# Window attention with a 3x3 depthwise position term: value-first slot order, earlier projection, and 30 channels convolved two blocks ahead

## The chip, the cores and the metric

The kernel runs on one core of a Trainium2 chip. The metric is the device time of one execution in microseconds (us). The core has five engines with queues of their own that work in order: TensorE (PE in the profile, with weight loads shown as PEld), VectorE (DVE), ScalarE (ACT), GpSimd (POOL) and SyncE (SP). Here SP only issues DMA transfers. Engines wait for one another through semaphores.

## The reference, cut to what matters

The input is an image of 511 x 511 positions with 192 channels in bfloat16. It is cut into 73 x 73 windows of 7 x 7 = 49 positions, and attention with 4 heads of 48 channels runs inside each window.

```python
pe = jnp.zeros_like(x)
for i in range(kk):                  # kk = 3, zero padding of 1
    for j in range(kk):
        pe = pe + xp[:, i:i + H, j:j + W, :] * dw_pe[i, j][None, None, None, :]
x0 = x + pe
h = _layernorm(x0, axis=-1)
...                                  # 73 x 73 windows of 49 positions
qkv = (hw @ w_qkv).reshape(-1, ws * ws, 3, nh, dh)
attn = jnp.einsum('wnhd,wmhd->whnm', q, k) * scale
attn = _softmax(attn, axis=-1)
out = jnp.einsum('whnm,wmhd->wnhd', attn, v)
out = out.reshape(-1, ws * ws, C) @ w_o
...
return x0 + out
```

## The kernel before

**Blocks.** Windows lie on partitions: up to 128 of them make a block. `_blocks` lists "halves" of 64 windows, two to a block. The first 73 halves are rows of windows (columns 0 to 63). The next 9 are columns of windows (columns 64 to 72, window rows 0 to 63). The 9 x 9 windows of the remaining corner make a last, smaller block. That gives 42 blocks: 0 to 35 of row halves, 36 with one of each, 37 to 40 of column halves, and 41 the corner with 81 windows.

**Tiles of a block.** `XP` (one buffer) holds the padded 9 x 9 patch of every window, 81 partitions x 128 windows x 192 channels. `X` (three buffers, block b in `X[b % 3]`) holds the 49 positions of every window; the convolution is added to it in place, later the attention's result, and it is stored from there. `HO` (two buffers) holds the normalized input with channels on partitions, and later, in the same place, the attention's output. `h` (two buffers) is the normalized input of seven positions before its transpose.

**Work for block b+1, done while block b is in attention.** Convolution: one matmul for each channel, `XP` against a table `T` (81 x 49) of that channel's weights, into `psc` (L314); after ten channels DVE adds the result to `X` (L320). Normalization, in seven rows of seven positions: statistics on DVE (L325), then on POOL a scale (L334), a power of -0.5 (L335) and the product (L337), which gives `h`. Then 14 transposes on TensorE into two `psc` buffers (L347), copied to `HO` by DVE and ACT (L357).

**Attention, in slots.** A slot handles one group of eight windows; a full block has 16 slots, the corner block 11. The letters are those of the code:

- A (`stage_A`, twice): q, then k, matmuls L369 into `ps`, each copied by ACT (L377), which is where most convolution matmuls are mixed in, by `fill`
- E (`stage_E`): transposes the result of two slots ago (L452), copied to `HO` by DVE (L453)
- `proj`: output projection of the block before, four positions at a time, 13 for a block (L464). ACT copies it to `pO` (L475, L477) and POOL adds it to `X` (L479)
- the transposes L347 of the next block, if one is due
- D (`stage_D`): the attention weights of the slot before times v (L428); DVE takes the reciprocal of the sums and scales (L437, L438)
- B (`stage_B`): scores (L407), whose exponential ACT writes to `pt` (L415)
- V (`stage_V`): v for this slot (L385), copied by ACT (L393)

The order of this list is the order of the slot, and all engines' queues are filled in that order (the schedule is written out by hand). `ps` has three buffers and `psc` two, each taken in rotation.

**Due times.** In the main loop, f is the share of the block's slots that is done at the end of a slot, and `part(lo, hi, total)` says how much of a list of `total` pieces is due when f goes from `lo` to `hi`. Convolution, projection, statistics, transposes, `XP` loads and `X` loads of block b+2 each have such a pair. `hook(share)`, called at five places in a slot, issues what is due of the statistics, stores and loads. Stores of a block's rows follow its projections. All loads and stores are issued on SP's queue: `XP` at L236 (nine patch columns for each half, more where a half touches the image's edge and is cut), clears of padding at L198, `X` at L250, stores at L299. `XP` loads for block b+2 start only when the convolution of block b+1 is done.

**Start.** `XP` is set to zero, weights are folded and a check of the logits' size is computed, the first loads are placed, and a branch picks `fast` (the path that runs) or `slow`. `fast` then convolves and normalizes block 0 before the first slot.

Of the kernel before, what the change touches and what calls it, by code (L numbers as in the profile page):

```python
# [41 lines left out]
def _blocks(nwr, nwc):  # L42

    full, tall = min(_HALF, nwc), min(_HALF, nwr)
    halves = [(a, 0, 0, 1, full) for a in range(nwr)]
    halves += [(0, b, 1, 0, tall) for b in range(full, nwc)]
    blocks = [[h + (64 * i,) for i, h in enumerate(halves[k : k + 2])] for k in range(0, len(halves), 2)]
    if nwc > full:
        cur, p = (blocks.pop(), 64) if len(halves) % 2 else ([], 0)
        for a in range(tall, nwr):  # L50
            n = nwc - full
            if p + n > BLK:
                blocks.append(cur)
                cur, p = [], 0
            cur.append((a, full, 0, 1, n, p))
            p += n
        if cur:
            blocks.append(cur)
    return blocks


class _Kernel:
    def __init__(self, ctx, tc, x, dw_pe, w_qkv, w_o, out, eps, logit_lim):
# [12 lines left out]
        nc.vector.memset(self.XP[:, 0:88, :], 0.0)  # L76
        nc.gpsimd.memset(self.XP[:, 88:BLK, :], 0.0)
        self.ident = consts.tile([128, 128], BF, name="ident")
        self.zero = consts.tile([16, C], BF, name="zero")
        nc.vector.memset(self.zero[:], 0.0)  # L80
        self.T = big.tile([128, C, S], BF, name="T")
        self.X = [big.tile([128, S, C], BF, name=f"X{i}") for i in range(3)]
# [3 lines left out]
        gi = consts.tile([1, 1], I32, name="gi")  # L86

# [89 lines left out]
        counts = [max(ln[4] + ln[5] for ln in blk) for blk in _blocks(self.NWR, self.NWC)]  # L177
        for i, t in enumerate(self.X):
            if len(counts) <= i or counts[i] < BLK:
                nc.gpsimd.memset(t[:], 0.0)  # L180
        for t in list(self.load_xp(0)) + list(self.load_x(0)):
            t()
# [19 lines left out]
    def load_xp(self, b):  # L202

        nc, x, XP, XPr, W, NWR, NWC = self.nc, self.x, self.XP, self.XPr, self.W, self.NWR, self.NWC
        blocks, clear, dram = _blocks(NWR, NWC), self.clear, self.dram
        for a0, b0, da, db, n, p0 in blocks[b]:
            left = [0] if b0 == 0 else []
            right = [] if b0 + (n - 1) * db < NWC - 1 else list(range(n)) if da else [n - 1]
            if left and any(ln[1] for bb in blocks[:b] for ln in bb):
                yield clear(XPr[0], p0, n if da else 1)  # L210
            if right and b:
                yield clear(XPr[8], p0 + right[0], len(right))
            last = a0 + (n - 1) * da
            cuts = [0] + ([1] if da and a0 == 0 else []) + ([n - 1] if da and last == NWR - 1 else []) + [n]
            for i, j in zip(cuts, cuts[1:]):
                if j <= i:
                    continue
                top, bot = a0 + i * da == 0, a0 + (j - 1) * da == NWR - 1
                if top and b:
                    yield clear(XP[0:9], p0 + i, j - i)  # L220
                if bot and b:
                    yield clear(XP[KP - 9 : KP], p0 + i, j - i)
                pr0, pr1 = (1 if top else 0), (8 if bot else 9)
                for pc in range(9):
                    q, sh = (WS - 1, -1) if pc == 0 else (0, 1) if pc == 8 else (pc - 1, 0)
                    n0, n1 = i, j
                    if pc == 0 and left:
                        n0 = j if da else i + 1
                    if pc == 8 and right:
                        n1 = i if da else j - 1  # L230
                    if n1 <= n0:
                        continue
                    dims = [[W * C, pr1 - pr0], [WS * C * (W * da + db), n1 - n0], [1, C]]
                    dst = XPr[pc, pr0:pr1, p0 + n0 : p0 + n1, :]
                    src = dram(x, WS * (a0 + n0 * da) - 1 + pr0, WS * (b0 + n0 * db + sh) + q, dims)
                    yield lambda dst=dst, src=src: nc.sync.dma_start(out=dst, in_=src)  # L236
# [7 lines left out]
    def load_x(self, b):  # L244

        nc = self.nc
        for r0, r1 in ((0, 4), (4, WS)):
            for p, at in self.strips(b, r0, r1):
                dst = self.X[b % 3][p, r0 * WS : r1 * WS, :].rearrange("p (r q) c -> p r (q c)", q=WS)
                yield lambda dst=dst, src=self.dram(self.x, *at): nc.sync.dma_start(out=dst, in_=src)  # L250


    def fast(self, ctx):
# [7 lines left out]
        tmp1 = pool.tile([128, S], F32, name="tmp1")  # L261
        expo = pool.tile([128, S], F32, name="expo")
# [3 lines left out]
        v_ = pool.tile([128, 4, NH, S], BF, name="v")  # L266
# [7 lines left out]
        for t in (pt, v_):  # L274
            nc.vector.memset(t[:], 1.0)
# [54 lines left out]
        def ln_norm(b, r, eng):  # L330

            t = slice(r * WS, (r + 1) * WS)
            e = nc.gpsimd
            e.tensor_scalar(out=tmp1[:, t], in0=bnst[:, t, 2], scalar1=1.0 / C, scalar2=self.eps, op0=ALU.mult, op1=ALU.add)  # L334
            e.tensor_tensor(out=rstd[:, t], in0=tmp1[:, t], in1=expo[:, t], op=ALU.pow)  # L335
            h = hr.next()
            eng.tensor_tensor(  # L337
                out=h[:], in0=self.X[b % 3][:, t, :], in1=rstd[:, t].unsqueeze(2).to_broadcast([128, WS, C]), op=ALU.mult
            )
            return h  # L340
# [38 lines left out]
        def stage_V(b, ck, fill, eng):  # L379
# [39 lines left out]
        def stage_D():  # L419
# [68 lines left out]
        class Next:  # L488
# [16 lines left out]
            def stats(n_, goal):  # L505
                while n_.si < goal and len(n_.ready) - n_.tr < 2:
                    n_.items[n_.si]()
                    n_.si += 1
# [19 lines left out]
        sq = []  # L528

        for g in range(NG + LE + 1):  # L530
# [6 lines left out]
            if ck == 0:  # L537
                n = Next(b + 1) if b + 1 < NB else None
# [8 lines left out]
            if 1 <= b and ck >= LE:  # L547
                goal = 13 if b == NB else part(0.10, 0.68, 13)
# [4 lines left out]
            conv_goal = part(0.0, 0.45, C)  # L553
# [10 lines left out]
            s_goal = part(0.46, 0.83, len(n.items)) if n else 0  # L564

            def hook(share):
# [3 lines left out]
                if n and conv.c == C:  # L570
# [5 lines left out]
                if conv is None or conv.c == C:  # L576
                    goal = part(0.45, 0.82, len(xp), at)
# [3 lines left out]
                    if b < 1 or stored.get(b - 1, 0) == len(CHUNKS):  # L581
                        goal = part(0.80, 0.90, len(xl), at)
# [9 lines left out]
            if g < NG:  # L592
                stage_A(b, ck, 1, fill)
                hook(0.35)
            for s0 in pj:
# [4 lines left out]
            hook(0.55)  # L600
            now[0] = g + 0.5
            if n and g < NG:
                n.transpose(part(0.57, 0.95, WS), 0.9)
            if 0 <= g - LD < NG:
                stage_D()
            if g < NG:
                stage_B()
                hook(0.75)
                stage_V(b, ck, fill, nc.scalar.copy)
                if n:  # L610
                    while conv.c < conv_goal:
                        conv_mm(conv)
# [263 lines left out]
```

## Time and profile before

Median of three runs: 4291.93 us (4291.89 to 4298.81). The profiled execution spans 4282.5 us.

| what | value |
|---|---|
| PE busy | 3637.9 us (85%) |
| ACT busy | 2779.9 us (65%) |
| DVE busy | 2548.2 us (60%) |
| POOL busy | 2061.2 us (48%) |
| mean granted TensorE clock | 0.910 |
| DMA traffic | 376.91 MB, 88 GB/s on the mean |
| first exponential, end of block 0's preparation | 107.4 us |
| one projection add on POOL (L479) | 1565 ns |
| one norm on POOL (L334, L335, L337) | 208, 1485 and 2432 ns |

The page gives busy time by engine, then the span in 40 slices, in which the row PEclk is the TensorE clock that the throttle granted in tenths of full speed. A row of the waits view reads: engine, line, what it waited for, us in total, times, longest. A row of the order of time reads: start, length, engine, line, operation, out<-in, and in brackets the idle time before it with what ended it. "issue" is idle time in which the engine waited for nothing that the profile shows.

### The profile page before, as it was taken

Reading aid. Unit: us, or ns where it says so; the run is one execution under the profiler, and the core shown is the slowest. Engines: PE = TensorE matmul, PEld = TensorE weight load, DVE = VectorE, ACT = ScalarE, POOL = GpSimd, SP = SyncE. Lnnn points to the kernel's source line nnn. Section 1 sums busy time; section 2 is a strip of 40 time slices with the busy share of each in tenths; the row PEclk is TensorE's granted clock in tenths of the full one; section 3 lists DMA queues with packets and bytes.
Section 4 is the critical chain, followed back from the end, with each engine's and each line's share of the span. In section 5 each row is a group of like instructions: output and inputs, shape, how many; then the busy total and the mean of one; then the engine's idle time right before and its main releaser. Section 6 shows DMA issues by size and latency. Waiting matters only on the chain.

```text
span 4282.5 us, 166362 instructions
## 1 busy us (share of the span) xinstructions
PE 3637.9 (85%) x75049; PEld 3180.5 (74%) x75049; DVE 2548.2 (60%) x4238; ACT 2779.9 (65%) x3508; POOL 2061.2 (48%) x1428
## 2 busy tenths in 40 slices
PE   4888888888989898888888888888889987777867
PEld 3777777777777787777777777777777876666656
DVE  6665666665565666666566566666656655555534
ACT  1666676666666677767666666766766665555646
POOL 4244455554444455555444445555544444444434
PEclk9998999999898899999999899999988997888878
DMA  5233344444333334444333333444433333333211
GB/s 121 62 85 85 91 97 97 105 102 99 84 85 85 85 91 95 103 107 104 91 85 85 85 91 91 98 98 104 106 86 85 85 84 84 84 84 71 54 43 43
DMA packets 522734, 376.91 MB, mean 88 GB/s; under 512 B 447216, under 2 KB 447408, under 8 KB 522014
## 3 DMA queue, kind: packets, MB, share of 16 engines
q1 hardware_dynamic: 521548, 365.89, 37.3%
q8 instruction: 589, 9.65, 0.9%
q14 instruction: 131, 1.07, 0.1%
q10 hardware_dynamic: 466, 0.30, 0.0%
HBM read 265.31 MB, written 100.27 MB: 85 GB/s over the span
## 4 chain that ended last, share of the span: by engine, by line
PE 51%; POOL 15%; DVE 10%; ACT 9%; SPq 6%; issue 5%; DMA 3%; ACTq 0%; POOLq 0%; DVEq 0%
PE ps L369 17%; PE psc L314 10%; PE ps L385 8%; POOL h L337 6%; ACT pO L475 6%; PE ps L452 6%; SPq L236 5%; POOL X L479 4%; PE ps L464 4%; POOL rstd L335 4%; DVE o L438 3%; PE psc L347 3%; DMA X<-in_x_dram 3%; DVE bnst L325 2%; ACT k L377 2%
## 5 line engine op out<-in xcount | busy, mean ns | idle before, releaser
L479 POOL TENSOR_TENSOR X<-X,pO 128x768 bf16<-128x768 bf16 (+1 forms) x539 | 836.6, 1565 | 1855.5 <-ACT pO L475 1853.9
L369 PE MATMUL ps<-HO,Wqk 96*128 96x392 bf16 x5336 | 1454.5, 357 | 100.1 <-DVE o L438 91.0
L314 PEld LDWEIGHTS <-XP 81*128 81x128 bf16 x8064 | 1117.6, 176 | 254.0 <-issue 191.9
L314 PE MATMUL psc<-T,XP 81*128 81x49 bf16 x8064 | 1100.6, 220 | 141.4 <-DMA XP<-in_x_dram 53.9
L377 ACT CAST k<-ps 128x784 bf16<-128x784 f32 x667 | 541.8, 812 | 477.9 <-PE ps L369 456.1
L369 PEld LDWEIGHTS <-Wqk 96*128 96x128 bf16 x5336 | 605.3, 117 | 261.5 <-issue 159.6
L385 PE MATMUL ps<-Wv,HO 96*128 96x192 bf16 x5336 | 687.5, 259 | 122.9 <-ACT pO L475 95.4
L377 ACT CAST q<-ps 128x784 bf16<-128x784 f32 x667 | 544.0, 816 | 316.2 <-PE ps L369 266.5
L453 DVE COPY HO<-ps 96x784 bf16<-96x784 bf16 x667 | 381.9, 573 | 614.9 <-PE ps L452 551.2
L320 DVE TENSOR_TENSOR X<-psc,X 128x490 bf16<-128x490 f32 x840 | 541.4, 645 | 321.6 <-PE psc L314 257.6
L337 POOL TENSOR_TENSOR h<-X,rstd 128x1344 bf16<-128x1344 bf16 x291 | 707.7, 2432 | 22.8
L393 ACT CAST v<-ps 128x768 bf16<-128x768 f32 x667 | 536.7, 805 | 234.8 <-PE ps L385 211.8
L438 DVE TENSOR_TENSOR o<-ps,rs 128x768 bf16<-128x768 f32 x667 | 638.7, 958 | 23.5
L415 ACT ACTIVATE pt<-ps 128x784 bf16<-128x784 f32 x667 | 550.9, 826 | 124.1 <-PE ps L407 121.0
L385 PEld LDWEIGHTS <-HO 96*128 96x128 bf16 x5336 | 520.7, 107 | 122.5 <-issue 94.0
L357 DVE COPY HO<-psc 96x896 bf16<-96x896 bf16 x294 | 339.0, 1153 | 323.8 <-PE psc L347 322.1
L325 DVE BATCH_NORM_STATS2 bnst<-X 128x6 f32<-128x384 bf16 x1050 | 518.1, 547 | 3.0
L452 PEld LDWEIGHTS <-o 128*96 128x96 bf16 x5336 | 422.1, 137 | 53.8 <-issue 8.6
L452 PE MATMUL ps<-ident,o 128*96 128x128 bf16 x5336 | 456.2, 234 | 3.9 <-issue 2.5
L464 PE MATMUL ps<-Wo,HO 96*128 96x192 bf16 x4116 | 454.2, 260 | 0.8 <-DVE HO L453 0.7
L357 ACT COPY HO<-psc 96x896 bf16<-96x896 bf16 x294 | 324.1, 1102 | 194.1 <-PE psc L347 152.1
L335 POOL TENSOR_TENSOR rstd<-tmp,expo 128x7 f32<-128x7 f32 x294 | 436.7, 1485 | 24.5
(54 smaller groups left out, 2872.0 us busy)
## 6 DMA issues: line engine op xcount, KB each, us to landing
XP<-in_x_dram SPq DMA_DIRECT2D x568, 216.0 KB
out_dram<-X SPq DMA_DIRECT2D x246, 336.0 KB
X<-in_x_dram SPq DMA_DIRECT2D x82, 672.0 KB
X<-in_x_dram SPq DMA_DIRECT2D x82, 504.0 KB
XP<-in_x_dram SPq DMA_DIRECT2D x151, 212.6 KB
out_dram<-X SPq DMA_DIRECT2D x82, 168.0 KB
XP<-in_x_dram SPq DMA_DIRECT2D x16, 192.0 KB
XP<-in_x_dram SPq DMA_DIRECT2D x64, 30.4 KB
```

Of the source, the lines that this page charges most:

```text
L314: mm(cv.ps[:, (c % 10) * S : (c % 10 + 1) * S], lhsT=XP[0:KP, :, c], rhs=T[0:KP, c, :], start=True, stop=True)
L325: nc.vector.bn_stats(out=bnst[:, s : s + 2, :].rearrange("p a f -> p (a f)"), in_=self.X[b % 3][:, s : s + 2, :].rearrange("p s c -> p c s"),)
L335: e.tensor_tensor(out=rstd[:, t], in0=tmp1[:, t], in1=expo[:, t], op=ALU.pow)
L337: eng.tensor_tensor(out=h[:], in0=self.X[b % 3][:, t, :], in1=rstd[:, t].unsqueeze(2).to_broadcast([128, WS, C]), op=ALU.mult)
L357: eng(out=HO[b % 2][0:KT, kt, :, r * WS : (r + 1) * WS], in_=pb[kt][:, 0 : WS * 128].rearrange("p (s w) -> p w s", w=128),)
L369: mm(ps[:, ab * 512 : ab * 512 + TOK], lhsT=self.Wqk[kt][0:KT, which * 2 + ab, :], rhs=HO[b % 2][0:KT, kt, ck * CH : (ck + 1) * CH, 0:S], ...
L377: nc.scalar.copy(out=dst[:, :, 0:TOK], in_=two_bank(ps, TOK))
L385: mm(ps[:, col : col + C], lhsT=HO[b % 2][0:KT, kt, w : w + 2, :].rearrange("p w s -> p (w s)"), rhs=self.Wv[kt][0:KT, :], start=(kt == 0) ...
L438: nc.vector.tensor_tensor(out=o_[:].rearrange("p b q (h d) -> p b (q h) d", d=DH), in0=ov[:, :, :, 0:DH], in1=r_[:].rearrange("p (b g) -> ...
L452: mm(ev, lhsT=o_[:, sl, Q, kt * KT : (kt + 1) * KT], rhs=ident[:], start=True, stop=True, is_transpose=True)
L464: mm(ps[:, col : col + C], lhsT=HO[b % 2][0:KT, kt, :, s0 + i], rhs=self.Wo[kt][0:KT, :], start=(kt == 0), stop=(kt == 1))
L479: nc.gpsimd.tensor_tensor(out=xv, in0=xv, in1=o[:, 0:n, :], op=ALU.add)
```

## The change

It rearranges the schedule; the arithmetic stays, except for how padding is cleared at the start. Its parts:

1. **Slot order.** V moves ahead of the projections and gets two `v` buffers, since D of the slot before now comes after it. The transposes move to the end of the slot, behind B.
2. **Due times.** Projection is due over 0.10 to 0.56 of the block (was 0.68), convolution to 0.39 (was 0.45), statistics 0.40 to 0.76 (were 0.46 to 0.83), transposes 0.51 to 0.88 (were 0.57 to 0.95), `XP` loads 0.38 to 0.66 (were 0.45 to 0.82), `X` loads 0.62 to 0.82 (were 0.80 to 0.90).
3. **Convolution two blocks ahead.** When all else is done for block b+1, the last slots convolve up to 30 channels of block b+2. This uses slots that held little work.
4. **X loads in rows.** A full block's `X` comes in 14 transfers, one for each of seven pixel rows and each half, instead of four.
5. **Column halves** cover window rows 1 to 64, so that they don't touch the image's edge and need no cut; the corner block takes window rows 0 and 65 to 72.
6. **Start.** `XP` is no longer set to zero as a whole; its padding is cleared by small transfers. The first loads are placed before the setup. Block 0's norms use `X[2]` as seven `h` buffers, so that they need not wait for transposes.

```diff
-    halves += [(0, b, 1, 0, tall) for b in range(full, nwc)]
+    halves += [(top, b, 1, 0, tall) for b in range(full, nwc)]
...
-        nc.vector.memset(self.XP[:, 0:88, :], 0.0)
-        nc.gpsimd.memset(self.XP[:, 88:BLK, :], 0.0)
...
+        for t in list(self.load_xp(0)) + list(self.load_x(0)):
+            t()
...
-            if right and b:
+            if right:
...
-        for r0, r1 in ((0, 4), (4, WS)):
+        for r0, r1 in [(r, r + 1) for r in range(WS)] if len(_blocks(self.NWR, self.NWC)[b]) <= 2 else [(0, WS)]:
...
-            h = hr.next()
+            h = self.X[2][:, t, :] if b == 0 else hr.next()
...
-                while n_.si < goal and len(n_.ready) - n_.tr < 2:
+                while n_.si < goal and len(n_.ready) - n_.tr < (2 if n_.b else WS):
...
-                goal = 13 if b == NB else part(0.10, 0.68, 13)
+                goal = 13 if b == NB else part(0.10, 0.56, 13)
...
-            conv_goal = part(0.0, 0.45, C)
+            conv_goal = (EARLY if b else 0) + part(0.0, 0.39, C - (EARLY if b else 0))
+            if n and conv.c == C and n.tr == WS and nn and xpn == len(xp) and xln == len(xl):
+                conv, conv_goal = nn.conv, part(0.875, 1.0, EARLY)
...
-            s_goal = part(0.46, 0.83, len(n.items)) if n else 0
+            s_goal = part(0.40, 0.76, len(n.items)) if n else 0
...
-                    goal = part(0.45, 0.82, len(xp), at)
+                    goal = part(0.38, 0.66, len(xp), at)
...
-                        goal = part(0.80, 0.90, len(xl), at)
+                        goal = part(0.62, 0.82, len(xl), at)
...
+                stage_V(b, ck, fill, nc.scalar.copy, vv[g % 2])
+                while n and conv.c < conv_goal:
+                    conv_mm(conv)
+                hook(0.55)
             for s0 in pj:
                 proj(b - 1, s0, b == NB and s0 % 8 == 0)
...
-            hook(0.55)
-            now[0] = g + 0.5
-            if n and g < NG:
-                n.transpose(part(0.57, 0.95, WS), 0.9)
             if 0 <= g - LD < NG:
-                stage_D()
+                stage_D(vv[(g - LD) % 2])
             if g < NG:
                 stage_B()
+                now[0] = g + 0.5
                 hook(0.75)
-                stage_V(b, ck, fill, nc.scalar.copy)
                 if n:
-                    while conv.c < conv_goal:
-                        conv_mm(conv)
+                    n.transpose(part(0.51, 0.88, WS), 1.0)
                     hook(1.0)
```

## The prediction

> **What bounds the kernel now.** I read the page first, then the stretches view cut by block, then what TensorE waits for, then the order of time around the longest waits.
>
> ```profile
> PE 3637.9 (85%) x75049; PEld 3180.5 (74%) x75049; DVE 2548.2 (60%) x4238; ACT 2779.9 (65%) x3508; POOL 2061.2 (48%) x1428
> PEclk9998999999898899999999899999988997888878
> PE 51%; POOL 15%; DVE 10%; ACT 9%; SPq 6%; issue 5%; DMA 3%; ACTq 0%; POOLq 0%; DVEq 0%
> ```
>
> TensorE bounds it, at a clock that is not full, and the chain leaves it for POOL (15%), for "issue" (5%), and for the SP queue and DMA (9%). These are the leaks to be priced. In the stretches view (columns: PE, weight loads, DVE, ACT, POOL, clock, DMA share, GB/s) the first two rows are whole row blocks, the next two end to end inside such a block, then the end of a block, then a column block and the block in which the corner block's rows are fetched:
>
> ```profile
> 1758.60:1849.00 90.40, 80.80 (x1799) 72.10 (x1800) 58.33 (x98) 66.07 (x84) 48.84 (x34) 1.00 0.43 100
> 2138.60:2237.20 98.60, 86.66 (x1799) 76.28 (x1799) 59.93 (x101) 66.77 (x85) 48.82 (x34) 0.93 0.40 92
> 2199.30:2202.70 3.40, 1.05 (x16) 0.71 (x14) 0.21 (x2) 0.97 (x2) 3.24 (x5) 1.00 0.70 191
> 2202.70:2209.50 6.80, 6.80 (x103) 5.16 (x102) 4.75 (x8) 4.28 (x5) 6.25 (x5) 0.54 0.74 198
> 2215.00:2227.00 12.00, 7.44 (x164) 5.75 (x153) 6.39 (x11) 6.72 (x8) 6.74 (x5) 0.86 1.03 198
> 3734.00:3849.80 115.80, 88.00 (x1798) 76.37 (x1798) 59.72 (x100) 66.26 (x85) 48.84 (x34) 0.83 0.37 80
> 3965.20:4103.70 138.50, 87.66 (x1797) 76.57 (x1797) 59.80 (x100) 67.11 (x84) 48.82 (x34) 0.80 0.22 49
> ```
>
> Both row blocks hold 1,799 matmuls; one takes 90.4 us at clock 1.00, the other 98.6 at 0.93. The 34 row blocks (0 to 33) fill 107.4 to 3407.2 us, so 3299.8/34 = 97.05 us each. The third row is a hole (PE 1.05 of 3.40 us), and the next 6.8 us run at about half clock. What makes the holes:
>
> ```profile
> PE psc L347 <- POOL h L337: 83.8, 66, 2.4
> PE ps L407 <- issue: 49.8, 15, 4.5
> PE ps L428 <- issue: 19.0, 12, 2.4
> ...
> 2194.43 3.24 POOL L479 TENSOR_TENSOR X<-X,pO 128x768 bf16<-128x768 bf16 x2
> 2199.50 2.43 POOL L337 TENSOR_TENSOR h<-X,rstd 128x1344 bf16<-128x1344 bf16 x1
> 2201.99 0.98 PE L347 MATMUL psc<-ident,h 128*96 128x128 bf16 x14 [2.35 <-POOL h L337]
> 2212.08 3.25 SPq L250 DMA_DIRECT2D X<-in_x_dram  x4
> 2224.07 0.26 PE L407 MATMUL ps<-q,k 48*64 48x49 bf16 x5 [4.02 <-issue]
> ```
>
> First hole: in every row block the third transpose waits 2.35 us for h, because two projection adds (3.24 us) stand before that norm on POOL. Second hole: near the end of nearly every block TensorE stops 2 to 4 us inside a run of matmuls, with no semaphore to wait for ("issue"), while the four X loads, issued within 3.25 us, hold the DMA share at 1.03 for 12 us.
>
> [...] The page's instruction queue q8 agrees (589 packets, 9.65 MB: 16.4 KB each)[...]. So I read the second hole as a fetch held up behind the X loads; the trace shows the coincidence, not the cause.
>
> **The change, part by part.**
>
> Slots. A row block has 16 slots (groups of 8 windows). From the planner's fractions I wrote out what falls where. Before: projections P0 to P12 in slots 2 to 10, norms N0 to N6 in slots 8 to 13, transposes in slots 9 to 15 ahead of D and B, conv 27 channels a slot in slots 0 to 6, then 5. After: P0 to P12 in slots 2 to 8, norms in 7 to 12, transposes in 8 to 14 at the slot's end, conv 26 a slot in 0 to 5, then 6, and 30 channels of the block after next in slot 15. TensorE's instructions are the same in number; only their places move.
>
> First hole. POOL's queue after, counted from the start of slot 6, with 1.6 us an add (L479: 1565 ns) and 0.21 + 1.49 + 2.43 = 4.13 us a norm: P8 and P9 done by 7, N0 13, P10 14, N1 18, P11 and P12 21, N2 25, N3 29, N4 33, N5 38, N6 43 us. At some 5.3 us a slot the transposes come up at 17, 23, 28, 33, 38, 44, 49 us: each h is 4 us early or more. The hole goes: 2.35 us.
>
> Second hole. X loads become 14 issues of 7 short rows each, due over 0.62 to 0.82 of the block (slots 10 to 13, some 17 us) where four were due over 0.80 to 0.90 (slot 13). 2.36 MB over 17 us is 139 GB/s; the loads ran at about 214 alone (stretch 2219.90:2224.10: 216). DMA no longer saturates for long, so fetches are not held: 2 to 4 us go. The price is 10 more SP issues a block, at 0.27 (the smallest L250 issue) to 0.65 us (its median): 3 to 6.5 us of a queue that issues for some 30 of 97 us. Cost nothing; idle SP time hides it. The stores still wait for POOL's last add (21 us above, slot 9), and X loads stand behind them; the wait ends before slot 10.
>
> Clock. Without holes the two half-clock spells of a block go too. The 1.00-clock block took 90.40 us and still held the 2.35 us h wait and no long fetch hole: 90.40 - 2.35 = 88.05. I take 88.0 us a row block. 34 x (97.05 - 88.0) = 308 us.
>
> V first. V now needs the ps buffer that A's first half filled, released by the q cast. After B, ACT runs exp 0.83, a transpose copy 1.05, q cast 0.81: 2.7 us. TensorE meanwhile runs transpose 0.95, A 0.85, E 0.61, A 0.85: 3.26 us. So nothing; with the whole cast exposed it would be 0.81 us a slot, which I keep for a rival. In return A's first half no longer waits for DVE's o (91.0 us in all before), and k's cast has V to hide behind. In slots with four statistics DVE does 1.97 + 0.25 + 0.96 + 1.10 + 0.57 = 4.85 us against TensorE's 4.94, so a few tenths remain; such slots existed before too. The second v buffer only removes a write-after-read wait.
>
> Two blocks ahead. 30 channels in slot 15 fill a slot that was light, and slots 0 to 5 lose one channel each. They read XP and X for block b+2; in row blocks the last issue falls about slot 13, near 70 us, and lands by 80, against slot 15 at 82. Nothing lost.
>
> Column blocks. Moving the column halves to window rows 1 to 64 removes the cut at the top edge: 18 XP loads instead of 36, and no clears in most. In the block at 3734 the SP queue spent 15.4 + 5.6 + 2.0 + 19.7 = 42.7 us on 36 XP issues, of which 18 are small (about 0.67, together 12), so a tall one costs 1.7. It started at 3787 and reached X only at 3836, and conv then stood still for two waits. After: 18 x 1.7 = 31, stores 5.4, X 14 x 0.35 = 5, in all 41 us from slot 6 (37 us): done near 78, or 82 with the wait on stores[...]. The early conv in slot 15 may wait a little: I take 90 us. Blocks 35 to 38 took 109.5, 120.0, 115.8, 115.4 = 460.7, so 460.7 - 360 = 101 us saved.
>
> Block 39 fetches the corner block: 81 XP loads and 10 clears before, 81 and 11 after, about 0.80 us each. SP issues for 9 x 0.35 + 92 x 0.80 + 8 stores x 0.6 = 82 us from about 37: it ends at 119, and the early conv in slot 15 stands until then. With 8 us for the rest of the slot at half clock: 127 against 138.5, 11 us saved. Blocks 34 and 40 (97.2, 99.0) gain what row blocks gain, 9 us each.
>
> Start and end. The memset of XP (7.10 us on DVE, first in its queue) is gone and loads start at once: setup ends 7 us earlier, weights competing with bulk loads may give some back. Block 0's normalization (60.7 to 102 us) stays a POOL-DVE chain: all statistics now precede the seven HO copies on DVE, which then cost 7 x 1.75 us in a row: I work out 43 us against 41. Net -5. The end (30.4 us after the last exp) is the same.
>
> Sum: 308 + 101 + 11 + 18 + 5 = 443; 4292 - 443 = 3849, say **3850 us**.
>
> **Rivals.** *One hole stays* (28%): the fetch hole moves along with the X loads, or the early conv waits for X in slot 15, each with a half-clock spell. For it: X loads wait behind XP and stores on one in-order queue and may bunch; I inferred the cause of the hole. [...] Half of the 9 us a block comes back, 39 blocks x 4.5 = 176: 4026 us. *The order costs more than the holes* (10%): V waits out the q cast in every slot. For it: three ps buffers rotate, and ACT is 65% busy. Against: the 3.26 to 2.7 us above. 667 slots x 0.81 = 540: 4390 us, slower than now. *The waits only change names* (2%): POOL, DVE and fetch lose together what the clock gains, about 4290.
>
> **How the numbers follow.** My forecast has 60%: 3850. The low end takes row blocks at 86 (34 x 2 = 68) and a shorter corner wait (20): 3760. The high end takes in "one hole stays" with a little more: 4070. Faster 0.88, same 0.03, slower 0.09.
>
> **What would show it.** Right: PEclk near 1.0 through the row blocks, the L347 wait on L337 gone from TensorE's list, no "issue" hole over 1.5 us with a DMA share of 1 beside it, row blocks at 88 us, column blocks at 90, one long conv wait only in block 39. Wrong: half-clock spells still twice a block, TensorE waiting at V for the q cast or in slot 15 for DMA, or POOL's norms again behind adds.

## The result, and the profile after

The changed kernel takes **3891.83 us** (median of three runs, 3889.15 to 3905.86), against 4291.93 before: a ratio of **0.9072, 95% interval 0.9036 to 0.9108** (ratios here are of mean times). In experiments 2 and 7 one run each was over 1.5% slower than the fastest of its kernel: the ratios leave it out, the medians keep it. The forecast was 3850 with a range of 3760 to 4070. The profiled execution spans 3887.3 us, at a mean clock of 0.973 where it was 0.910.

The page of the kernel after, its busy times, its clock row and its chain by engine:

```profile
PE 3422.5 (88%) x75049; PEld 3029.4 (78%) x75049; DVE 2519.8 (65%) x4238; ACT 2799.0 (72%) x3508; POOL 2049.4 (53%) x1427
PEclk9799999999999999999999999999999999999888
PE 31%; DVE 13%; ACT 7%; DMA 4%; SPq 3%; issue 2%; POOL 1%; ACTq 0%; POOLq 0%; DVEq 0%
```

The same 75,049 matmuls keep TensorE busy 215 us less, at the fuller clock. In the clock row two places stand out: the second slice (block 0), and the last three slices (from about 3596 us on: blocks 39, 40 and the corner). In the chain POOL goes from 15% to 1%, "issue" from 5% to 2%, SPq from 6% to 3%. (The shares named here add up to 61% only, so I read which ones left, not what the rest is.)

The stretches view of the kernel after (columns: PE, weight loads, DVE, ACT, POOL, clock, DMA share, GB/s): a row block, 12 us of it while its X loads land, a column block, block 39, and the time before block 0's first exponential:

```profile
2393.40:2480.80 87.40, 80.36 (x1796) 71.62 (x1796) 59.21 (x100) 66.86 (x84) 48.70 (x34) 1.00 0.43 103
2456.00:2468.00 12.00, 10.33 (x227) 7.93 (x228) 9.72 (x17) 10.22 (x13) 10.03 (x7) 1.00 0.91 197
3477.10:3575.30 98.20, 84.26 (x1797) 73.24 (x1797) 59.25 (x101) 67.10 (x84) 48.67 (x34) 0.91 0.40 92
3575.30:3719.10 143.80, 84.89 (x1799) 73.88 (x1799) 59.22 (x101) 67.07 (x85) 48.69 (x34) 0.79 0.23 47
0.00:111.70 111.70, 43.66 (x427) 40.35 (x428) 66.67 (x95) 17.49 (x18) 43.46 (x27) 0.99 0.50 118
```

A row block now runs at clock 1.00 with PE busy 80.4 of 87.4 us. In those 12 us the DMA share is 0.91 (1.03 in the hole before), and the clock stays full (1.00). Over the busiest 12 us of each row block's X loads the share has a median of 0.94, and 1.05 before. The column block and block 39 still lose clock and PE time, and the start takes longer than before (107.4). What TensorE waits for after, over the whole span (us in total, times, longest):

```profile
PE ps L429 <- DVE HO L454: 110.3, 205, 1.0
PE ps L370 <- ACT pO L476: 69.7, 234, 1.4
PE psc L315 <- DMA XP<-in_x_dram: 40.3, 1, 40.3
PE psc L315 <- DVE X L321: 36.3, 7, 12.6
PE psc L315 <- DMA X<-in_x_dram: 36.1, 12, 16.0
PE psc L315 <- DVE HO L358: 27.9, 28, 1.0
...
PE ps L386 <- ACT q L378: 20.1, 86, 0.4
PE psc L348 <- POOL h L338: 14.7, 37, 0.5
...
PE ps L408 <- issue: 2.9, 4, 1.2
```

The two holes are gone from the list: the wait for POOL's h has fallen to 0.5 us at the longest, and "issue" before the scores to 2.9 us in all (49.8 before). The list is now headed by D (L429) behind DVE and A (L370) behind ACT, in many short pieces, and by convolution (L315), which waits for a `psc` buffer (27.9 us) and for loads, these in few and long pieces at the start and from block 34 on. The short waits have changed names but not shrunk: in row blocks 3 to 33, waits of up to 1 us come to 5.8 us a block before and 5.7 after, and longer ones to 4.9 before and 0.9 after.

Cut by block (a block runs from its first exponential to the next block's), predicted and measured in the profiled execution. As in the prediction, the "column blocks" 35 to 38 are those during which the blocks of column halves, 37 to 40, are loaded:

| stretch | before | predicted | after |
|---|---|---|---|
| start, to the first exponential | 107.4 | 102.4 | 111.7 |
| row blocks 0 to 33 | 3299.8 | 2992 | 2983.3 |
| block 34 | 97.2 | 88.2 | 95.4 |
| column blocks 35 to 38 | 460.7 | 360 | 384.9 |
| block 39 | 138.5 | 127 | 143.7 |
| block 40 | 99.0 | 90 | 84.0 |
| corner block and end | 79.8 | 79.8 | 84.2 |

Row blocks 3 to 33 take 87.63 us on the mean (97.07 before). Their clock is 0.997 (0.921), and TensorE stands still for 7.3 us of each (10.9). So of 9.4 us, 3.6 are idle time that went, and 5.8 are busy time of the same matmuls, at the fuller clock. Half-clock spells (stretches at clock 0.50, in steps of 3.413 us) start 8 times in blocks 2 to 40, where it was 70 times.

### The profile page after: what moved, and what is told of

Same layout as the page of the kernel before. It is cut to its first block, busy times and chain, and to the rows that moved or that the text cites. A ratio compares the mean times of both kernels' runs of the same rounds, so it can differ in the third digit from the quotient of the medians.

```text
span 3887.3 us, 165790 instructions
## 1 busy us (share of the span) xinstructions
PE 3422.5 (88%) x75049; PEld 3029.4 (78%) x75049; DVE 2519.8 (65%) x4238; ACT 2799.0 (72%) x3508; POOL 2049.4 (53%) x1427
## 3 DMA queue, kind: packets, MB, share of 16 engines
q14 instruction: 126, 1.03, 0.1%
## 4 chain that ended last, share of the span: by engine, by line
PE 31%; DVE 13%; ACT 7%; DMA 4%; SPq 3%; issue 2%; POOL 1%; ACTq 0%; POOLq 0%; DVEq 0%
PE ps L370 10%; PE psc L315 6%; ACT pO L476 5%; PE ps L386 5%; DVE bnst L326 4%; PE ps L465 4%; PE ps L453 4%; DMA X<-in_x_dram 4%; DVE HO L358 3%; DVE o L439 3%; ACT v L394 2%; SPq L238 2%; PE ps L429 2%; DVE HO L454 1%; DVE rs L438 1%
## 5 line engine op out<-in xcount | busy, mean ns | idle before, releaser
L370 PE MATMUL ps<-HO,Wqk 96*128 96x392 bf16 x5336 | 1379.3, 338 | 90.0 <-ACT pO L476 69.7
L315 PEld LDWEIGHTS <-XP 81*128 81x128 bf16 x8064 | 1108.6, 176 | 195.3 <-issue 100.7
L315 PE MATMUL psc<-T,XP 81*128 81x49 bf16 x8064 | 1061.1, 217 | 140.7 <-DMA XP<-in_x_dram 40.3
L370 PEld LDWEIGHTS <-Wqk 96*128 96x128 bf16 x5336 | 565.6, 112 | 153.6 <-issue 38.9
L386 PE MATMUL ps<-Wv,HO 96*128 96x192 bf16 x5336 | 643.5, 247 | 26.7 <-ACT q L378 20.1
L438 DVE RECIPROCAL rs<-ps 128x16 f32<-128x16 f32 x667 | 171.3, 257 | 692.6 <-PE ps L429 545.2
L336 POOL TENSOR_TENSOR rstd<-rstd,expo 128x7 f32<-128x7 f32 x294 | 435.4, 1481 | 24.5
L453 PEld LDWEIGHTS <-o 128*96 128x96 bf16 x5336 | 377.3, 128 | 76.5 <-DVE o L439 39.7
L465 PE MATMUL ps<-Wo,HO 96*128 96x192 bf16 x4116 | 435.7, 258 | 0.7 <-DVE HO L454 0.7
L453 PE MATMUL ps<-ident,o 128*96 128x128 bf16 x5336 | 425.2, 223 | 4.5 <-DVE o L439 3.1
L476 ACT CAST pO<-ps 128x768 bf16<-128x768 f32 x498 | 387.3, 801 | 40.9 <-PE ps L465 25.2
```

Of the source, the lines that this page charges most:

```text
L315: mm(cv.ps[:, (c % 10) * S : (c % 10 + 1) * S], lhsT=XP[0:KP, :, c], rhs=T[0:KP, c, :], start=True, stop=True)
L370: mm(ps[:, ab * 512 : ab * 512 + TOK], lhsT=self.Wqk[kt][0:KT, which * 2 + ab, :], rhs=HO[b % 2][0:KT, kt, ck * CH : (ck + 1) * CH, 0:S], ...
L386: mm(ps[:, col : col + C], lhsT=HO[b % 2][0:KT, kt, w : w + 2, :].rearrange("p w s -> p (w s)"), rhs=self.Wv[kt][0:KT, :], start=(kt == 0) ...
L453: mm(ev, lhsT=o_[:, sl, Q, kt * KT : (kt + 1) * KT], rhs=ident[:], start=True, stop=True, is_transpose=True)
L465: mm(ps[:, col : col + C], lhsT=HO[b % 2][0:KT, kt, :, s0 + i], rhs=self.Wo[kt][0:KT, :], start=(kt == 0), stop=(kt == 1))
L476: nc.scalar.copy(out=o[:].rearrange("p (b s) c -> p b (s c)", b=2), in_=two_bank(ps, 2 * C))
```

## Experiments

Row-block figures are means of blocks 3 to 33 of a profiled execution; ratios are to the kernel before on the same chip, with 95% intervals. Single blocks are less steady than the means: in a second profile of the changed kernel (experiment 10) row blocks take 87.71 us, and blocks 34 to 38 take 96.9, 99.1, 99.2, 99.2 and 98.6.

**1. The old slot order in the changed kernel.**

```diff
-                stage_V(b, ck, fill, nc.scalar.copy, vv[g % 2])      # ahead of proj
...
+                n.transpose(part(0.51, 0.88, WS), 0.9)               # after proj, ahead of D and B
...
-                    n.transpose(part(0.51, 0.88, WS), 1.0)           # after B
+                stage_V(b, ck, fill, nc.scalar.copy, vv[g % 2])      # after B
```

> The changed kernel with the slot order of before (transposes ahead of D, V last), all else as changed. Theory 'two holes' (row blocks gained because two holes in TensorE's work and the half-clock spells behind them are gone): the new due times alone still give POOL time, so no hole returns and row blocks stay at 88 to 89 us: 3900 to 3940 us. Rival 'order' (the gain comes from casts that hide behind V): most of the 9.6 us a row block is lost, 4100 to 4200 us.

Measured: 4016.12 us, 0.9387 (0.9341 to 0.9432), between the two expectations. Row blocks take 90.67 us, 3.0 more, with 9.3 us idle at clock 0.988. TensorE's waits in it:

```profile
PE ps L370 <- DVE o L439: 146.3, 285, 0.8
PE psc L348 <- POOL h L338: 93.0, 81, 1.5
PE ps L408 <- ACT k L378: 45.1, 97, 0.8
```

These are the waits of the kernel before, back under their old names: A's first half behind DVE's o, B behind the cast of k, and the transposes behind POOL's h, though the new due times are all in place. So, with the rest of the change in place, the order is worth some 3 us a row block, which my sum had at nothing, and it is part of why the POOL hole went. V and the transposes move together here, so the two are not told apart.

**2. Old due times for projection, statistics and transposes, and no convolution two blocks ahead.**

```diff
-        EARLY = 30
+        EARLY = 0
-                goal = 13 if b == NB else part(0.10, 0.56, 13)
+                goal = 13 if b == NB else part(0.10, 0.68, 13)
-            s_goal = part(0.40, 0.76, len(n.items)) if n else 0
+            s_goal = part(0.46, 0.83, len(n.items)) if n else 0
-                    n.transpose(part(0.51, 0.88, WS), 1.0)
+                    n.transpose(part(0.57, 0.95, WS), 1.0)
```

> The changed kernel with the due times of before for projection, statistics and transposes, and without the convolution two blocks ahead (which would not fire then). Theory 'two holes', with POOL's queue counted as in the prediction: the transposes at the slot's end leave each h 2 us early or more, so the wait for h stays away; X loads start one slot later and are a little closer together: 3890 to 3960 us. Rival 'due times alone close the POOL hole': it returns with its half-clock spell, 4.45 us a row block, about 4040 us.

Measured: 4207.17 us (4176.02 to 4239.04), 0.9811 (0.9745 to 0.9876). Both expectations missed it, by far. Row blocks take 95.55 us, yet TensorE is idle only 7.4 us of each: the loss is clock (0.894). Three views of it: a wait and, in order of time, one case of it, then two stretches, the half-clock spell that follows it and a block without one.

```profile
PE ps L370 <- DVE HO L358: 49.5, 42, 1.2
```

```profile
1939.09 0.34 PE L370 MATMUL ps<-HO,Wqk 96*128 96x392 bf16 x1 [1.20 <-DVE HO L358]
```

```profile
1940.56:1978.11 37.55, 37.55 (x533) 31.89 (x532) 17.07 (x27) 16.77 (x21) 4.92 (x3) 0.50 0.01 2
2136.80:2226.40 89.60, 81.75 (x1797) 71.71 (x1797) 59.44 (x101) 67.06 (x85) 48.74 (x34) 1.00 0.38 101
```

With the old due time the seventh transpose is the last work of slot 15, and A of the next block, which comes right behind it, needs its copy: 1.2 us once a block (42 times). Then TensorE runs at half clock for 37.55 us, 11 steps of 3.413 us, in which TensorE is busy without a gap by the profile. A block without the spell takes 89.60 us. Experiments 3 and 4 put back the projections' time or take out the early convolution alone, and neither has this wait: it comes from the times of statistics and transposes. So in this order the earlier due times chiefly keep A at the block's boundary from waiting; the hole at POOL, for which I had credited them, doesn't come back (26.8 us in all, 0.8 at the longest).

**3. Only the projections' due time put back.**

```diff
-                goal = 13 if b == NB else part(0.10, 0.56, 13)
+                goal = 13 if b == NB else part(0.10, 0.68, 13)
```

> The changed kernel with one due time put back: projections P0 to P12 due over 0.10 to 0.68 of a block instead of 0.10 to 0.56, all else as changed. Theory (the first hole is POOL's norms standing behind projection adds, and it went because the projections now end two slots earlier): the wait of a transpose for POOL's h comes back at one place a block, 1 to 2.4 us with a half-clock spell of one or two windows behind it (up to 3.4 us lost), so row blocks go from 87.6 to 90 to 93 us, and the time to 3980 to 4080 us. Rival (putting the transposes at the end of a slot, with norms due from 0.40, already gives POOL enough lead; the projections' due time is worth nothing by itself): no POOL wait over 1 us, row blocks within 0.5 us of 87.6, time 3880 to 3910 us.

Measured: 3923.9 us, 0.9172 (0.9127 to 0.9216), beside 0.9117 (0.9083 to 0.9151) of the changed kernel on the same chip. In row blocks no wait for POOL's h is over 0.6 us, which speaks for the rival. But they take 88.88 us, 1.2 more, and neither theory had the reason. The order of time between the exponentials of slots 10 and 11, and the stretch behind it:

```profile
1859.26 0.44 PE L429 MATMUL ps<-v,pt 49*64 49x49 bf16 x32 [0.87 <-DVE HO L454]
...
1860.26 1.54 PE L348 MATMUL psc<-ident,h 128*96 128x128 bf16 x14 [0.30 <-POOL h L338]
```

```profile
1860.50:1863.91 3.41, 3.41 (x27) 2.72 (x25) 2.98 (x5) 2.26 (x3) 3.25 (x4) 0.50 0.82 220
```

Small waits, 0.87 and 0.30 us and others, come to a median of 1.24 us of idle time between these two exponentials. In most row blocks one or two steps of 3.41 us at half clock follow (the "windows" of the expectation). In the changed kernel no such interval has a median over 1.14 us, and the clock nearly always stays full (0.997 in row blocks).

**4. No convolution two blocks ahead.**

```diff
-        EARLY = 30
+        EARLY = 0
```

> The changed kernel without the 30 channels two blocks ahead. TensorE is the bound in every slot, so in row blocks the place of these matmuls does not matter: 87.4 us stays within 0.5. In the column blocks and in the block that loads the corner, convolution no longer stands in slot 15 waiting for DMA: 5 us less in each of six blocks, so 3850 to 3890 us. Rival 'the light slot 15 was worth filling': row blocks lose 2 us or more, 3960 us.

Measured: 3932.02 us, 0.9193 (0.9149 to 0.9236). Row blocks 87.95 us, 0.3 more, as expected. In the column blocks the expectation was wrong: blocks 34 to 36 gain 2 to 4 us each (91.8, 92.0, 93.9), but 37 to 40 take 109.1, 105.8, 151.0 and 101.9 us where the changed kernel takes 96.5, 98.2, 143.7 and 84.0 (in the second profile 99.2, 98.6, 144.5 and 84.1). The stretch of block 38:

```profile
3480.70:3586.50 105.80, 97.28 (x1797) 81.18 (x1797) 59.70 (x101) 67.41 (x84) 48.74 (x34) 0.77 0.36 86
```

PE is busy 97.28 of 105.8 us: again clock (0.77) more than waiting. Without the early channels the wait for loads falls at the block's boundary, and spells of 13 steps and more then run through the convolution slots. Convolving early moves the wait into slot 15, where it costs less.

**5. X loads bunched again.**

```diff
-        for r0, r1 in [(r, r + 1) for r in range(WS)] if len(_blocks(self.NWR, self.NWC)[b]) <= 2 else [(0, WS)]:
+        for r0, r1 in ((0, 4), (4, WS)):
-                        goal = part(0.62, 0.82, len(xl), at)
+                        goal = part(0.80, 0.90, len(xl), at)
```

> The changed kernel with X loaded in four large transfers due over 0.80 to 0.90 of a block, as before. Theory 'fetch behind bursts': the DMA share goes back to 1.0 for some 12 us late in each block, the hole of 2 to 4 us without a semaphore and a half-clock spell come back, some 5 us a row block: about 4060 us. Rival (the hole had another cause, such as the light slots at the end of a block): no such hole, 3890 to 3910 us.

Measured: 4063.95 us, 0.9491 (0.9445 to 0.9537); row blocks 91.62 us, 4.0 more, clock 0.957. This is what the theory expected. In TensorE's waits the row that had gone is back, near its old size:

```profile
PE ps L408 <- issue: 43.5, 14, 4.5
```

**6. X loads in rows, in the kernel before.**

```diff
-        for r0, r1 in ((0, 4), (4, WS)):
+        for r0, r1 in [(r, r + 1) for r in range(WS)] if len(_blocks(self.NWR, self.NWC)[b]) <= 2 else [(0, WS)]:
-                        goal = part(0.80, 0.90, len(xl), at)
+                        goal = part(0.70, 0.90, len(xl), at)
```

> The kernel before, with X loaded in 14 row transfers due over 0.70 to 0.90 of a block, and nothing else. Theory 'fetch behind bursts': the hole without a semaphore late in the block and its half-clock spell go, 5 us a row block, while the 2.35 us wait for h stays: 4290 - 170 = 4120 us. Rival 'only spreading over earlier slots helps, which needs the early projection': 4270 us or more, since X then lands later.

Measured: 4112.89 us, 0.9616 (0.9578 to 0.9654); row blocks 92.50 us, 4.6 less. This too is what the theory expected. Its waits keep the POOL hole and lose the "issue" one:

```profile
PE psc L347 <- POOL h L337: 122.4, 85, 7.1
...
PE ps L407 <- issue: 2.0, 3, 1.3
```

Experiments 5 and 6 take the same part out of one kernel and put it into the other, and find 4.0 and 4.6 us. That X loads in a few large transfers, issued close together, make the second hole is shown; whether their size or their closeness does it is not told apart.

The traces' DMA records also show what TensorE lacks in this hole. The queue of kind "instruction" moved 589 packets of 16,384 bytes, and TensorE ran 150,279 weight loads and matmuls, 255 for each packet. In the kernel before, blocks 1 to 39, 26 stops named "issue" are longer than 1.5 us. In every one of them a packet of this queue lands, 1.25 to 1.73 us before the stop ends; and each of the 26 falls after the same number of TensorE's instructions, counted modulo 256, while the 51 stops of that length with another name fall at some 50 different counts. In experiment 5 all 19 such stops fall at that same count. I read this as TensorE standing until the next packet of its instructions came; the records show where the stops fall and when the packets land, and no more. How bunched X loads would delay that packet is not shown.

**7. Filling the first hole with dummy work, in the kernel before.** Eleven matmuls on old data, whose result is overwritten, stand ahead of the third transpose.

```diff
+                for _ in range(11 if b and r == 2 and kt == 0 else 0):
+                    mm(raw[:, 0:TOK], lhsT=self.Wqk[0][0:KT, 0, :], rhs=HO[(b + 1) % 2][0:KT, 0, 0:CH, 0:S], start=True, stop=True)
```

> The kernel before, with 11 extra matmuls (96x392, about 0.21 us each, 2.3 us together, their results overwritten) put right ahead of the third transpose of each block, where TensorE waits 2.35 us for h. Theory 'half clock is the larger part of a hole': TensorE does not look idle, the half-clock spell behind this hole stays away, and though work is added each block gets about 2.1 us shorter: 41 blocks, some 85 us less than before, ratio 0.98. Rival 'a hole costs its own length and no more': ratio 1.00. Rival 'the extra work adds up': 2.3 us more a block, ratio 1.02.

Measured: 4252.41 us, 0.9934 (0.991 to 0.9959): a little faster with more work, by a third of what was expected. The wait for POOL's h falls from 122.3 us in all to the row below, and no block has a spell at this place any more; from the exponential of slot 10 to that of slot 12, 13.28 us become 11.58. At the block's end, from slot 14's to that of the next slot 2, 26.86 us become 28.42, because the spells there last longer (14.6 us a block at half clock, 9.8 before).

```profile
PE psc L350 <- POOL h L337: 48.1, 85, 7.1
```

So the clock does fall because of that hole: with the wait filled, no spell follows there. But a spell saved in one place isn't always saved for good.

**8. Column halves at window rows 1 to 64, in the kernel before.**

```diff
+    top = min(1, nwr - tall)
-    halves += [(0, b, 1, 0, tall) for b in range(full, nwc)]
+    halves += [(top, b, 1, 0, tall) for b in range(full, nwc)]
-        for a in range(tall, nwr):
+        for a in [*range(top), *range(top + tall, nwr)]:
```

> The kernel before, with the column halves moved to window rows 1 to 64 and nothing else. Theory 'issue-bound column blocks': 18 issues instead of 36, some 12 us less of SP's queue, so blocks 35 to 38 fall from 115 us to 103; row blocks stay at 97: about 55 us less, ratio 0.987. Rival 'the transfers, not the issues, set it': ratio 0.998 or more.

Measured: 4227.85 us, 0.9883 (0.9835 to 0.9932), as the theory expected. SP issues for 38 to 42 us in each of these blocks, where it was 50 to 57. Blocks 35 to 38 take 99.1, 98.9, 107.3 and 106.8 us, 48.6 less than before of the 75.8 that the whole change saves there.

**9. Three repairs in the changed kernel:** fewer X loads for block 0, its norms two at a time, and the corner's X loads ahead of most of its XP loads.

```diff
+        rows = [(0, 4), (4, WS)] if b == 0 else [(r, r + 1) for r in range(WS)]
-                while n_.si < goal and len(n_.ready) - n_.tr < (2 if n_.b else WS):
+                while n_.si < goal and len(n_.ready) - n_.tr < 2:
-                        goal = part(0.62, 0.82, len(xl), at)
+                        goal = part(0.62, 0.82, len(xl), at) if b + 2 < NB - 1 else part(0.52, 0.56, len(xl), at)
```

> The changed kernel with three edits: block 0's X in four transfers instead of 14, block 0's norms two at a time as before, and the corner block's X loads due right after the stores instead of behind its 81 XP loads. If the missed parts of my sum are rightly placed: first exponential 5 to 8 us earlier, and the second stop of 12.6 us in the block that loads the corner gone, 3870 us (ratio to the changed kernel 0.995). If XP's landing alone sets that stop: 3885 us.

Measured: 3908.97 us, 0.9133 (0.9101 to 0.9165): no gain. The start is 110.8 us, 0.9 less and not 5 to 8: convolution goes on later still (at 47.61 us, after 9.17 us behind X), so the landing of X and not its 14 issues sets that wait, and the time from there to the first exponential is 2.7 us shorter. In block 39 (145.3 us) two waits have become one, in order of time; the second row is of SP's own waits:

```profile
3721.17 0.35 PE L316 MATMUL psc<-T,XP 81*128 81x49 bf16 x2 [53.99 <-DMA XP<-in_x_dram]
...
SPq L238 <- DMA X<-in_x_dram: 8.2, 8, 1.7
```

53.99 us against 40.31 + 12.57 = 52.88: X had landed, but SP's issues take turns on eight semaphores (in the changed kernel's trace, 1,781 issues on eight numbers in rotation), and XP loads had waited 8.2 us for X loads to land. SP ended 129.0 us into the block, where it was 118.6.

**10. Fewer X issues in column blocks, wider X loads for the corner,** in the changed kernel; with it the changed kernel itself once more.

```diff
+            (a0, b0, _, _, n, p0), m = lines[1], len(lines) - 1        # the eight lower corner lines
+            for r in range(WS):                                        # one load a pixel row, 72 partitions
+                dst = self.X[b % 3][p0 : p0 + m * n, r * WS : (r + 1) * WS, :].rearrange("p s c -> p (s c)")
...
+        elif lines[0][2] or lines[-1][2]:
+            rows = [(0, 2), (2, 4), (4, 6), (6, WS)]
```

> The changed kernel with fewer or better spread X loads where SP's queue ends last: in blocks of column halves 8 X loads instead of 14 (rows in twos), and for the corner block the eight lower lines' X as 7 loads over 72 partitions each instead of 8 loads over 9 partitions. Theory (the waits in slots 14 and 15 of the column blocks are SP's issue time, 0.75 us an X load, and the corner's X wait is its slow landing over 9 partitions): column blocks 35 to 38 lose 6 x 0.75 = 4.5 us of waiting each and go from 96 to 91.5 to 93 us, block 39 loses the 12.6 us wait for X behind the XP wait of 40 us and goes from 143.7 to 131 to 134 us; together 25 to 30 us, time 3860 to 3870 us, ratio to the kernel before .899 to .903. Rival (the stops are set by the landing of the bytes or by the clock spells after them, not by the issues): columns stay at 94 to 98 us, block 39 within 3 us, time 3885 to 3895 us.

> The changed kernel itself, unaltered, beside the other two on one chip, so that differences of half a per cent can be read: 3885 to 3900 us, row blocks 87.6, column blocks 94 to 98, block 39 143 to 145 us.

Measured: 3894.72 us, 0.9108 (0.9074 to 0.9141), and the changed kernel beside it 3898.29, 0.9117 (0.9083 to 0.9151): no difference that can be told. Block 39 takes 137.6 us instead of 144.5. Its second wait in order of time:

```profile
3724.70 0.20 PE L328 MATMUL psc<-T,XP 81*128 81x49 bf16 x1 [6.90 <-DVE X L334]
```

6.90 us where it was 11.8 on this chip, so part of the corner's X wait was indeed its landing. The column blocks didn't move: 35 to 38 take 393.2 us together against 396.1, since 8 larger loads keep SP for 8.0 to 10.8 us a block where 14 small ones took 10.3 to 11.8. There the rival held. None of the versions run beats the changed kernel.

## Why the prediction was right, and where its sum was off

**Row blocks: right, 87.63 against 88.0.** This is where 316 of the 395 us of the profiled spans come from. Both holes went, and their half-clock spells with them; the derivation from block 17 (90.40 - 2.35) met it within 0.4 us. It took for granted that nothing else in the block changes, and the short waits did come out even (5.8 and 5.7 us), though under other names.

**First hole: right outcome, the wrong part credited.** My working had POOL's queue clear earlier because projections end in slot 8 (by its own list each h is 3 us early or more, not 4: the third is done at 25 for 28). Experiment 3 puts that back, and h is still in time. Experiment 1 puts the order back, and waits of up to 1.5 us return; experiment 2, with the old due times in the new order, has 0.8 at most. So it is the new order, with V, D and B ahead of the transposes, that gives POOL its lead.

**Second hole: right.** It is worth 4.0 to 4.6 us a block with its spell (experiments 5 and 6), and the cause that was inferred, a late instruction fetch, fits where the stops fall, all 26 at one place in 256 (experiment 6). The cost was mis-sized without harm in row blocks: 14 X issues keep SP for 10.6 us, 0.75 each, where four took 3.5, so 7.1 more and not 3 to 6.5; SP has the idle time. (A block's X is 2.41 MB, 128 windows of 49 positions of 192 channels in 2 bytes, and not 2.36.)

**V first costs nothing: right.** V waits 20.1 us for the q cast in the whole span, 0.03 us a slot, where the rival had 0.81. The order's own gain of 3 us was missing from the sum. So were the short waits that it brings: D behind E's copy on DVE (110.3 us in all), for which I had said "a few tenths", and A's first half behind ACT's copy of the projection (69.7). They take the place of V behind that copy (108.4), A behind DVE's o (91.0) and B behind the cast of k (29.4). Of the rival "the waits only change names", this much came true.

**Two blocks ahead: right in row blocks, not in column blocks.** "Nothing lost" holds for the row blocks (0.3 us gained, after 0.8 us a block of new waits of the early convolution for a `psc` buffer). For column blocks I allowed that "the early conv in slot 15 may wait a little" and took 90 us. They took 94.1 to 98.2: the term is short by 25 us in all, and block 34, during which a block with one column half is loaded, by 7. TensorE waiting in slot 15 for DMA was named as a sign of being wrong, and there it does. The waits of block 38 after, in order of time, with the issues that they wait for:

```profile
3550.86 0.76 SPq L238 DMA_DIRECT2D XP<-in_x_dram  x1
3551.72 9.61 SPq L252 DMA_DIRECT2D X<-in_x_dram  x12
...
3558.42 0.36 PE L315 MATMUL psc<-T,XP 81*128 81x49 bf16 x2 [4.99 <-DMA X<-in_x_dram]
3566.09 0.20 PE L315 MATMUL psc<-T,XP 81*128 81x49 bf16 x1 [2.92 <-DVE X L321]
```

Two stops, 4.99 and 2.92 us, and spells behind them. The working took 14 x 0.35 = 5 us for X; it was 10.4 to 13.9 us. SP ended at 80 to 84 us into the block, near my own "78, or 82 with the wait on stores", since XP came a little cheaper. What failed is the step from there to the wait: I had slot 15 "at 82" and too little time for the landing. In this block slot 15 asks for its first load at 3553.43 (3558.42 - 4.99), 76 us in. The profile names X for that stop, but X and XP loads share semaphores, and a convolution matmul reads only `XP` and `T`: the last XP load, issued at 3550.86 behind two X loads, lands at 3558.18, 7.3 us later, and convolution goes on at 3558.42. In blocks 36 and 37 the first stop ends 0.2 us after that landing too. The second stop is X's: the last X load, issued by 3561.33, lets convolution go on only at 3566.09. So fewer X issues (experiment 10) had little to gain at the first stop. The two stops then cost clock as well (0.91 over the block).

**Block 39: wrong, 143.7 against 127.** SP's queue ended at 119 us, as worked out. The step "the early conv in slot 15 stands until then" forgot the landing. After, in order of time:

```profile
3692.55 0.36 PE L315 MATMUL psc<-T,XP 81*128 81x49 bf16 x2 [40.31 <-DMA XP<-in_x_dram]
3709.86 0.20 PE L315 MATMUL psc<-T,XP 81*128 81x49 bf16 x1 [12.57 <-DVE X L321]
```

40.31 us for XP were in the sum, 12.57 for X were not. The corner's X loads write 9 partitions each, and 1.52 MB landed in some 16 us, at 66 to 99 GB/s with a DMA share of 0.46 to 0.60. Why the share stays there is not shown; with the eight lower lines of the corner in loads of 72 partitions, this wait is 6.90 us where it was 11.8 on the same chip (experiment 10).

**Start: wrong sign, +4.3 instead of -5.** The setup did end earlier. But X is issued after XP, and the first convolution stops for it. In order of time, at the start:

```profile
30.58 9.99 SPq L252 DMA_DIRECT2D X<-in_x_dram  x14
45.77 15.54 PE L315 MATMUL psc<-T,XP 81*128 81x49 bf16 x172 [7.23 <-DVE X L321]
93.82 1.65 PE L348 MATMUL psc<-ident,X 128*96 128x128 bf16 x14 [23.68 <-DVE HO L358]
```

Convolution resumes at 45.77 us (45.36 before): what the setup gained is spent in the 7.23 us wait for X. The normalization then takes 65.9 us from there to the first exponential (62.0 before), as all statistics now stand ahead of the HO copies on DVE: a transpose waits 23.68 us for a `psc` buffer to be copied. I had seen that chain and taken 2 us for it; it cost 3.9. Experiment 9 undoes it and gets 2.7 back. Block 0 then runs at clock 0.77.

**Block 40 and the end** missed by -6 and +4.4 and nearly cancel: block 40 has no block two ahead, so it holds 30 channels less than the others. All stretches together are 48 us over the sum; that it is not 56 is luck, since row blocks came out 8.7 us under it.

**The clock.** The prediction took one spell of two steps (6.8 us) for each hole from the trace. At slot 10 that is mostly right (22 of the 31 row blocks). It is no rule: experiment 2 shows spells of 11 steps and more behind a shorter wait. There a step with 1.14 to 1.28 us of idle time was enough for a spell to follow, and ten steps busy throughout by the profile did not end one.

## What to carry to other kernels

When TensorE stops without a semaphore, count where in its instructions the stops fall: here all 26 fell at one place in 256, each with a packet of the instruction queue landing 1.25 to 1.73 us before its end (experiment 6). Price a short wait of TensorE by what the clock does after it (behind 1.20 us came 37.55 us at half clock in experiment 2), read the half-clock spell from the trace at that place, and move unavoidable waits to where a spell is short. Before crediting a due time with a gain, ask whether the order inside the step gives the same lead, and where the last item lands relative to the next block's first need. When small transfers feed a wait, add up issue time and landing time (7.3 us from the last XP issue to its landing in block 38), and count how many partitions each of them writes (a wait of 11.8 us with 9 a load, 6.90 with 72, in experiment 10).

## What was not expected of the hardware

- **Half-clock spells keep to a fixed grid, and a short wait falls into one step of it or is split.** In each of the 13 profiles (75 spells in the kernel before, 13 in the changed one) every spell starts on one grid of 3.413 us and, but for a last one cut off by the end, lasts a whole number of its steps. Counted over blocks 2 to 40 of all profiles, step by step at full clock: with less than 0.9 us of idle time in a step, 9 of 11,500 are followed by a spell; with 0.9 to 1.1 us, 25 of 446; with 1.1 to 1.5 us, 92 of 183; with 1.5 to 2 us, 80 of 84; with more, all 188. In experiment 2 the same 1.20 us wait brings no spell at 11 of the 30 boundaries behind blocks 3 to 32; there the step holds 1.05 to 1.20 us of idle time, and 1.14 to 1.28 where a spell follows.
- **How long a spell lasts is not set by the wait in these runs.** Behind some 1.24 us of idle time after slot 10, it is one or two steps (experiment 3); behind the wait at the block's boundary, 1 to 16, and in the case shown 11, 37.55 us with TensorE busy throughout by the profile (experiment 2). The long ones all run through slots in which convolution is mixed into A. Why these hold the clock down isn't settled here.
- **More work can be faster:** eleven matmuls in a hole took 0.4 to 0.9% off the time (experiment 7).
- **Single changes to row blocks don't add up.** Undone one at a time in the changed kernel they cost 4.0 us (X loads), 3.0 (order) and 7.9 (due times with early convolution), 14.9 together, where the whole change brings 9.4: undoing one can open a wait and spells that neither kernel has, as in experiment 2.
